# The last six sets of attention scores in two pairs of PSUM banks instead of one four-bank buffer, and a new list of the work

## The chip, the cores and the metric

The kernel runs on one core of one Trainium2 chip. The metric is the device time of one execution in microseconds (us), as the median of several runs. Beside it there is a profile of one execution; its span runs from the first to the last instruction. The engines are TensorE (PE in the profile; PEld is its loading of weights), VectorE (DVE), ScalarE (ACT), GpSimd (POOL) and SyncE (SP, which here only issues DMA transfers). Each of them works through its own instructions in the order in which they were issued.

## The reference

The input x has 2048 tokens of 640 features. Two attention layers of 32 heads with 20 features each read it, and a gate per token mixes their results.

```python
def reference(A_x, A_wqkv, A_w_phi, A_wo, B_x, B_wq, B_wk, B_wv, B_wo, B_beta, gate_w):
    ...
    # layer A: linear attention, features of a softmax of q and of -q
        phi_k = jnp.concatenate([_softmax(pk, axis=-1), _softmax(-pk, axis=-1)], axis=-1)
        kv = jnp.einsum('bhsf,bhsd->bhfd', phi_k, v)
        ...
        o = num / den
    ...
    # layer B: four segments of 512 tokens
        for s in range(N):
            ...
            logits = jnp.einsum('bhqd,bhkd->bhqk', qs, ks) * scale + mask
            p = _softmax(logits, axis=-1)
            a_dot = jnp.einsum('bhqk,bhkd->bhqd', p, vs)
            ...
            a_mem = num / den
            o = g * a_mem + (1.0 - g) * a_dot
            ...
            M = M + jnp.einsum('bhld,bhle->bhde', pk, vs)
    ...
    g = _sigmoid((x * gate_w).sum(-1, keepdims=True))
    return g * a + (1 - g) * b
```

## The kernel before, in words

**The list.** All work after the first loads is written as small steps in Python functions, and one long string, `ORDER` (line 847), says in which order they are issued. A word such as `P00` or `o1a` has a letter for the function (table `STEPS`, line 836), a digit for the step in it, and at the end a bank number or, with `a`, the wish that ScalarE does a copy in place of VectorE. How often a pair of letter and digit has come so far gives the number of the item, through the table `WHICH` where a step starts at another number or skips some. A helper (line 117) keeps each engine's instructions in the order of the list; that is why nearly all of the profile's rows carry line 117, and why they are told apart here by the names of their tiles. An engine that waits for something holds everything behind it.

**Layer B's attention** goes in groups of four heads: 4 segments of 8 groups, so groups 0 to 31. The scores of a pair of groups are computed as five sets (`scores`, line 595, letter `P`), 80 sets in all, numbers 0 to 79. A set fills four PSUM banks of 512 columns, one bank for each of four heads; keys stand on the 128 partitions and queries on the columns, and only the causal part is computed. Sets with number 0 or 3 in their five consist of one part, four matmuls with 32 rows (tile `st_ps`); those with 1, 2 or 4 consist of two parts, eight matmuls. Step 0 issues these matmuls, step 1 the exponential on ScalarE (tile `PT`, 128x2048), step 3 the causal masks on GpSimd (`affine_select` on `PT`): one mask in sets with number 0, 2 or 3 and two in those with 1 or 4.

There are eight banks. Four, with slots 0 to 3, are shared by all other work (`bank`, line 54). The other four begin as two pairs (`banks2`, line 61), which serve the folding of weights, the keys of layer A and the first three sets of scores (`NP = 3`); each of these sets has two exponentials of 1024 elements, steps 1 and 2, and its masks in steps 3 and 4. From set 3 on the four banks are one single buffer (`banks4`, line 64), so that the scores of one set wait until the exponential of the set before has read them.

The sums of the values weighted by `PT` (`attended_cols`, letter `U`, tile `uv_ps`) are turned by a DMA (`uN<-uT`) and normalized. In the last four groups (28 to 31, `UL = 28`) the letter `V` does it another way: forty matmuls with queries on the partitions (tile `nd_ps`; step 0 the part that needs no masks, step 4 the masked diagonal), normalized straight from PSUM (V1, V2, V3). `M` (memory) does the products with the running memory and adds both in `oB` (step 5).

**Layer A** projects q and k through weights into which the feature map is folded (`A`, `B`, `F`, `W`, and `f`, `d`, `n` for the queries: tiles `k_ps`, `v_ps`, `pf_ps`, `dn_ps`, `num_ps`). `k`, `K`, `v`, `q` are keys, features and values of layer B (`proj`, `q_ps`), and `Y` the features of its queries (`eq` on ScalarE). `T` turns x for the first 512 tokens, `L` lets a DMA do that for the others. `c` loads the ten parts of the output weights WoA and WoB, `l` turns 128 rows of both layers' results, and `o` does the output products of these rows (tile `o_ps`, ten matmuls for each half of 320 columns) and stores them.

**The tail.** The last 512 rows go another way. `t` and `b` turn layer A's and layer B's results at once (`b` in three transfers: the columns 0 to 383, 384 to 511, 512 to 639). For each block j of 128 rows, `p` does the products of the first three chunks of layer B, `a` all of layer A's, `e` and `z` those with the fourth and fifth chunk of layer B; `h` copies and stores. Blocks 0 and 3 use shared banks; blocks 1 and 2 use, as one four-bank tile `o2_ps` from `banks4`, the banks of the scores.

Of the kernel before, what the change touches and what calls it, by code (L numbers as in the profile page):

```python
# [7 lines left out]
ACT = mybir.ActivationFunctionType  # L8
# [7 lines left out]
def kernel(  # L16
# [29 lines left out]
    NP = 3  # L46

# [10 lines left out]
    early = ExitStack()  # L58
    ps2 = early.enter_context(tc.tile_pool(name="ps2", bufs=1, space=bass.MemoryType.PSUM))

    def banks2(name, slot):
        return ps2.tile([P, 2, 512], F32, name=name, tag=f"two{slot}", bufs=1)

    def banks4(name):
        if not hasattr(lt, "ps4"):
            early.close()
            lt.ps4 = ctx.enter_context(tc.tile_pool(name="ps4", bufs=1, space=bass.MemoryType.PSUM))
        return lt.ps4.tile([P, 4, 512], F32, name=name, tag="four", bufs=1)
# [526 lines left out]
    def scores(n, step, at, ev):  # L595
# [3 lines left out]
        if step == 0:  # L599
# [8 lines left out]
            if n < NP:  # L608
                pair = [banks2("st_ps", (at + u) % 2) for u in range(2)]
            else:  # L610
                t.ps = banks4("st_ps")
                pair = [t.ps[:, 0:2], t.ps[:, 2:4]]
# [7 lines left out]
        elif step < 3:  # L620
            if step == 1:
                t.all = bpt.tile([P, 4, 512], BF16, name="PT")
                t.PT = [t.all[:, 0:2], t.all[:, 2:4]]
            sca.activation(out=t.PT[step - 1] if n < NP else t.all,
                           in_=t.pair[step - 1] if n < NP else t.ps, func=ACT.Exp, scale=SCALE_B)
        else:
            PT, b = (t.PT[step - 3], 2) if n < NP else (t.all, 4)
            for v in ([PT.rearrange("p b (n q) -> p (b n) q", q=256)[:, :, 0:P]] if j == 2 else
                      [PT[:, :, d0:d0 + P] for d0 in ((0,) if j in (0, 3) else (0, 384))]):
                gps.affine_select(out=v, in_=v, pattern=[[0, 2 * b if j == 2 else b], [1, P]],  # L630
                                  compare_op=ALU.is_ge, fill=0.0, base=0, channel_multiplier=-1)
# [165 lines left out]
    def tail_mm(j, part, hs, at):  # L797
        t = item("tail", j)
        if part == 0 and j in (1, 2):
            if not hasattr(lt, "o2"):  # L800
                lt.o2 = banks4("o2_ps")
            t.ps = [lt.o2[:, 2 * j - 2 + h, 0:320] for h in range(2)]
# [23 lines left out]
    def tail_out(j, step, at, ev):  # L826
# [5 lines left out]
        else:  # L832
# [10 lines left out]
             **{f"M{j}": lambda i: i + G for j in range(2, 6)}, "p1": lambda i: 3 * i}  # L843
# [103 lines left out]
```

## Time and profile before

| | us |
|---|---|
| median of 3 runs | 287.55 (286.81 to 287.84) |
| profiled execution | 287.34 |
| its span | 285.6 |
| ScalarE: 77 exponentials of 128x2048 | 145.2 |
| ScalarE idle before these, waiting for scores | 14.9 |
| TensorE waiting for an exponential ahead of scores | 4.7 |

The times of the profile count from the start of the span. In the groups a row gives the busy time in total, the mean of one instruction in ns, and then the idle time of the engine just before such instructions with what ended most of it. In a timeline a row gives start, length, engine, the instruction, and in brackets how long the engine had been idle and what released it. The mean granted clock of TensorE is 0.998 of full speed.

By windows of the profile, columns being the stretch, its length, and the busy time and number of instructions on TensorE, of its weight loads, on VectorE, ScalarE and GpSimd, then clock, DMA share and GB/s:

```profile
250.00:260.00 10.00, 9.58 (x142) 6.89 (x134) 8.96 (x23) 8.34 (x6) 9.77 (x16) 1.00 0.53 107
260.00:270.00 10.00, 8.94 (x159) 6.32 (x156) 9.67 (x25) 9.04 (x7) 8.11 (x12) 1.00 0.67 139
270.00:280.00 10.00, 9.70 (x106) 7.19 (x106) 3.62 (x10) 2.63 (x3) 2.39 (x5) 1.00 0.13 29
280.00:285.60 5.60, 1.81 (x14) 1.08 (x11) 1.38 (x3) 0.93 (x3) 0.00 (x0) 0.88 0.33 117
```

### The profile page before, as it was taken

What the parts mean: (1) busy time and instruction counts of PE and PEld (TensorE: products, weight loads), DVE (VectorE), ACT (ScalarE), POOL (GpSimd) and SP (SyncE); (2) the same over time, 40 slices, a digit from 0 to 9 for tenths busy, and PEclk for the clock granted to TensorE, in tenths of its full rate; (3) what the DMA queues carried; (4) which work ended last, traced back from release to release, by engine and by line L of the source; (5) the groups of instructions that cost most, each with busy time, mean ns of one, the idle gap of its engine ahead of it and who ended that gap; (6) DMA issues with size and microseconds to landing.
All of it is one profiled execution on the core that took longest, in us unless ns stands there. A gap on an engine that the chain in (4) does not pass through costs nothing.

```text
span 285.6 us, 8511 instructions
## 1 busy us (share of the span) xinstructions
PE 272.6 (95%) x3371; PEld 173.4 (61%) x3393; DVE 237.2 (83%) x577; ACT 239.0 (84%) x259; POOL 183.0 (64%) x305
## 2 busy tenths in 40 slices
PE   7999999999999998999999999999999999999894
PEld 4777676677676545565556566455565556676673
DVE  5969999998889758999778989868999678999922
ACT  2489888897886999998998998999897997988902
POOL 8060000045445856798997799978899898999620
PEclk9999999999999999999999999999999999999999
DMA  7999960100111683356761624183474133564612
GB/s 223 282 239 210 147 149 22 37 2 2 39 21 25 167 116 76 70 108 118 136 97 39 142 63 102 51 128 80 90 83 98 22 92 74 110 118 79 153 38 92
DMA packets 79721, 28.11 MB, mean 98 GB/s; under 512 B 70081, under 2 KB 79681, under 8 KB 79681
## 3 DMA queue, kind: packets, MB, share of 16 engines
q1 hardware_dynamic: 78736, 26.84, 47.1%
q10 hardware_dynamic: 944, 0.74, 0.8%
q8 instruction: 26, 0.43, 0.6%
q14 instruction: 15, 0.11, 0.2%
HBM read 5.61 MB, written 2.62 MB: 29 GB/s over the span
## 4 chain that ended last, share of the span: by engine, by line
PE 67%; ACT 17%; DVE 6%; POOL 5%; issue 2%; DMA 1%; DVEq 0%; ACTq 0%
ACT PT L117 15%; PE proj L117 10%; PE o_ps L117 10%; PE v_ps L117 8%; PE k_ps L117 8%; PE st_ps L117 7%; PE pf_ps L117 5%; PE q_ps L117 5%; PE uv_ps L117 4%; POOL PT L117 2%; PE num_ps L117 2%; PE mem_ps L117 2%; POOL oA L117 2%; DMA WkB<-in_B_wk_dram 1%; PE zb_ps L117 1%
## 5 line engine op out<-in xcount | busy, mean ns | idle before, releaser
L117 ACT ACTIVATE PT<-st_ps 128x2048 bf16<-128x2048 f32 (+1 forms) x83 | 151.0, 1823 | 17.7 <-PE st_ps L117 15.7
L117 POOL TENSOR_SCALAR_AFFINE_SELECT PT<-PT 128x512 bf16<-128x512 bf16 (+2 forms) x116 | 78.9, 694 | 26.5 <-ACT PT L117 26.2
L117 PEld LDWEIGHTS <-xT 128*128 128x128 bf16 x640 | 59.9, 98 | 28.5 <-issue 4.3
L117 PE MATMUL st_ps<-qTp,kTs 32*128 32x384 bf16 (+3 forms) x512 | 31.8, 300 | 5.3 <-ACT PT L117 4.7
L117 ACT ACTIVATE Ek<-k_ps 128x640 bf16<-128x640 f32 x32 | 26.5, 893 | 5.3 <-PE k_ps L117 1.8
L117 POOL TENSOR_TENSOR oA<-t,t 128x320 bf16<-128x320 f32 x32 | 29.2, 914 | 1.3 <-DVE t L117 1.3
L117 DVE TENSOR_TENSOR t<-num_ps,dd 128x320 f32<-128x320 f32 x64 | 28.4, 478 | 0.8 <-PE num_ps L117 0.5
L117 POOL MEMSET qTp<- 128x4096 bf16 x1 | 3.5, 3512 | 39.3 <-ACT vA L117 39.3
L117 PEld LDWEIGHTS <-oT 128*128 128x128 bf16 x240 | 21.9, 98 | 9.8 <-issue 2.2
L117 PEld LDWEIGHTS <-kTs 32*128 32x128 bf16 (+1 forms) x552 | 14.9, 92 | 20.3 <-issue 16.0
L117 PE MATMUL proj<-WkB,xT 128*128 128x320 bf16 x160 | 25.7, 300 | 0.7 <-DVE xT L117 0.4
L117 PE MATMUL proj<-WvB,xT 128*128 128x320 bf16 x160 | 26.1, 300 | 0.0
L117 DVE TENSOR_REDUCE ksum<-Ek 128x64 f32<-128x1280 bf16 x16 | 23.1, 1455 | 2.4 <-ACT Ek L117 2.4
L117 PE MATMUL pf_ps<-xT,WqA 128*128 128x512 bf16 x91 | 24.3, 380 | 0.7 <-DVE uq L117 0.2
L117 PE MATMUL q_ps<-xT,WqB 128*128 128x512 bf16 x87 | 23.7, 380 | 0.9 <-issue 0.3
L117 PE MATMUL v_ps<-WvA,xT 128*128 128x320 bf16 (+1 forms) x160 | 24.2, 300 | 0.0
L117 PE MATMUL k_ps<-qTp,xT 128*128 128x320 bf16 x160 | 23.5, 299 | 0.0
L117 ACT ACTIVATE ET<-pf_ps 128x512 bf16<-128x512 f32 x40 | 21.9, 628 | 0.0
L117 POOL TENSOR_TENSOR oB<-td,tm 128x320 bf16<-128x320 f32 (+4 forms) x25 | 20.5, 824 | 1.2 <-DVE td L117 0.6
L117 DVE CAST uT<-uv_ps 128x512 bf16<-128x512 f32 x28 | 18.8, 670 | 2.4 <-PE uv_ps L117 2.2
L117 PE MATMUL uv_ps<-PT,vB 128*32 128x512 bf16 (+1 forms) x448 | 20.4, 302 | 0.2
L117 PE MATMUL o_ps<-WoA,oT 128*128 128x320 bf16 x120 | 20.3, 300 | 0.0
(114 smaller groups left out, 485.4 us busy)
## 6 DMA issues: line engine op xcount, KB each, us to landing
out_dram<-osb SPq DMA_DIRECT2D x12, 160.0 KB
qTp<-qd SPq DMA_DIRECT2D x8, 128.0 KB
WvB<-in_B_wv_dram SPq DMA_DIRECT2D x1, 800.0 KB
vA<-in_B_wq_dram SPq DMA_DIRECT2D x1, 800.0 KB
WvA<-in_A_wqkv_dram SPq DMA_DIRECT2D x1, 800.0 KB
WoA<-in_A_wo_dram SPq DMA_DIRECT2D x5, 160.0 KB
WoB<-in_B_wo_dram SPq DMA_DIRECT2D x5, 160.0 KB
qTp<-qd SPq DMA_DIRECT2D x8, 96.0 KB
```

What stands on the lines that cost most here:

```text
L117: return lambda *a, **k: kept(f(*a, **k))
```

## The change

The four banks now have three lives: two pairs for sets 0 to 2, one buffer of four banks for sets 3 to 73, and two pairs again for sets 74 to 79 (`NQ = 74`). The last six sets have two exponentials of 1024 elements each and their masks in halves (steps 3 and 4). The tail's blocks 1 and 2 take a pair each, slot 0 and slot 1, in place of the halves of one four-bank tile. `WHICH` gives the steps P2 and P4 the sets 0, 1, 2 and then 74 to 79. The list is written anew: it has six words each of P2 and P4 more, the bank numbers of 223 steps differ, and words have other places: among them the fourth turning of x (`T00`, ahead of the second projection of the keys), the loads of x (`L`), the ten loads of output weights (`c`, now all between set 11 and set 16), some projections, features and memory products around sets 4 to 33, and the order from set 69 to the end.

```diff
+    NQ = 74
...
-    def banks2(name, slot):
-        return ps2.tile([P, 2, 512], F32, name=name, tag=f"two{slot}", bufs=1)
+
+    def pool(part):
+        if part != pool.part:
+            if pool.part:
+                pool.now.close()
+            pool.part, pool.now = part, ctx.enter_context(ExitStack())
+            pool.ps = pool.now.enter_context(
+                tc.tile_pool(name=f"ps{part}", bufs=1, space=bass.MemoryType.PSUM))
+        return pool.ps
+
+    pool.part = 0
+
+    def banks2(name, slot, last=False):
+        return pool(3 if last else 1).tile([P, 2, 512], F32, name=name, tag=f"two{slot}", bufs=1)
...
+        return pool(2).tile([P, 4, 512], F32, name=name, tag="four", bufs=1)
+
+    def paired(n):
+        return n < NP or n >= NQ
...
-            if n < NP:
-                pair = [banks2("st_ps", (at + u) % 2) for u in range(2)]
+            if paired(n):
+                pair = [banks2("st_ps", (at + u) % 2, n >= NQ) for u in range(2)]
...
-            sca.activation(out=t.PT[step - 1] if n < NP else t.all,
-                           in_=t.pair[step - 1] if n < NP else t.ps, func=ACT.Exp, scale=SCALE_B)
-        else:
-            PT, b = (t.PT[step - 3], 2) if n < NP else (t.all, 4)
+            sca.activation(out=t.PT[step - 1] if paired(n) else t.all,
+                           in_=t.pair[step - 1] if paired(n) else t.ps, func=ACT.Exp, scale=SCALE_B)
+        else:
+            PT, b = (t.PT[step - 3], 2) if paired(n) else (t.all, 4)
...
-            if not hasattr(lt, "o2"):
-                lt.o2 = banks4("o2_ps")
-            t.ps = [lt.o2[:, 2 * j - 2 + h, 0:320] for h in range(2)]
+            o2 = banks2("o2_ps", at, True)
+            t.ps = [o2[:, h, 0:320] for h in range(2)]
...
+             **{f"P{j}": lambda i: i if i < NP else i - NP + NQ for j in (2, 4)}}
...
-        "T00 w0 T1 k01 T02 k1 T03 T1 T1 k00 T01 k1 k02 T1 k03 k1 k00 K0 K1 k1 k01 K2 k1 K0 k02 I0 "
+        "T00 w0 T1 k01 T02 k1 T03 T1 T00 T1 k01 T1 k1 k02 I0 k03 k1 k00 k1 K0 k01 K1 k1 K0 K2 k02 "
...
-        "n00 n13 o1 l0 M01 Y0 M5 P00 n2 o02 P1 Y1 P3 n3 M2 Y2 V00 n4 M3 o1a o2 V4 P3 U3 P00 M4 "
-        "M03 P1 o02 V1 U4 M2 U5 V2 M3 M5 o1 P00 P3 V3 o2 n01 P1 n12 M4 V00 n2 M5 V4 n3 n03 n11 V1 "
-        "n2 Y0 P00 V2 n4 n3 b0 o02 P1 Y1 P3 V3 Y2 n4 o1 Y0 Y1 P00 P3 t0 M03 P1 o01 Y2 M2 M00 M3 "
-        "o1 Y0 P3 P00 M4 V02 P1 M2 Y1 M5 V4 M3 o2 p01 Y2 p13 V1 P3 M4 P00 V2 P1 M00 V3 a0 M2 M5 "
-        "M3 p00 P3 b0 M4 V02 V4 p01 V1 V2 V3 a0 M5 b0 e0 e0 a0 p00 p12 z0 z1 e0 h0a h1 z0 z1 a0 "
-        "h0a h2 h1 h2 z0 z1 e0 h0a h1 z0 z1 h2 h0a h1 h2 ")
+        "M3 o01 P3 n2 n3 M4 n00 n4 n13 l0 o1 Y0 P00 Y1 o02 P1 P3 n2 n3 Y2 n4 V01 U3 o1 o2 V4 U4 "
+        "P00 P3 V1 M00 V2 P1 o03 U5 M2 M3 P2 M5 P00 o1 P3 V3 o2 n02 P1 M4 n13 P4 n01 n2 n10 M5 n3 "
+        "P2 V02 n2 V4 n3 P00 P3 b0 V1 o03 n4 V2 P1 P4 V3 P2 n4 P00 o1 P3 Y0 Y1 t0 o01 P1 P4 Y2 P2 "
+        "P3 P00 o1 Y0 Y1 P4 M00 P1 V02 Y2 o2 M2 V4 M3 M4 P2 p03 P3 V1 M5 p11 V2 Y0 P00 P4 Y1 M00 "
+        "P1 a0 V3 M2 Y2 P2 P3 M3 p00 P4 M4 V02 M5 V4 M00 p01 V1 M2 V2 M3 b0 V3 a0 M4 M5 b0 a0 e0 "
+        "p02 p10 e0 z0 z1 z0 h0a z1 h1 e0 h0a a0 h1 h2 h2 z0 z1 e0 h0a h1 z0 z1 h2 h0a h1 h2 ")
```

More of the change, by code (lines that the diff above doesn't have):

```diff
@@ L55, in bank @@
         return ps.tile(shape, dtype, name=name, tag=f"one{slot}", bufs=1)
-    early = ExitStack()
-    ps2 = early.enter_context(tc.tile_pool(name="ps2", bufs=1, space=bass.MemoryType.PSUM))
-    def banks2(name, slot):
-        return ps2.tile([P, 2, 512], F32, name=name, tag=f"two{slot}", bufs=1)
+    def pool(part):
[9 more added lines that the diff above has]
+        return pool(3 if last else 1).tile([P, 2, 512], F32, name=name, tag=f"two{slot}", bufs=1)
     def banks4(name):
[L65 to L68, printed above, removed]
+        return pool(2).tile([P, 4, 512], F32, name=name, tag="four", bufs=1)
+    def paired(n):
+        return n < NP or n >= NQ
     bres = ctx.enter_context(tc.tile_pool(name="bres", bufs=1))
@@ L842 @@
     WHICH = {**{f"V{j}": lambda i: i + UL for j in range(5)}, "k2": lambda i: 2 * i + 1, "o2": lambda i: 2 * i + 1, "S1": lambda i: 2 * i + 1,
-             **{f"M{j}": lambda i: i + G for j in range(2, 6)}, "p1": lambda i: 3 * i}
+             **{f"M{j}": lambda i: i + G for j in range(2, 6)}, "p1": lambda i: 3 * i,
+             **{f"P{j}": lambda i: i if i < NP else i - NP + NQ for j in (2, 4)}}
     ORDER = (
[61 rows of a table removed]
[61 rows of a table added]
     done = {}
```

108 rows, old and new, of the table ORDER are left out of this document.

## The prediction

> **What bounds the kernel now.** I read the page first, then the waits of TensorE, then the timelines of the last 30 us of TensorE, ScalarE, GpSimd and the DMA queue, then the groups by form, and last the stretch around 63 us, where the kernel before already works with pairs of banks.
>
> ```profile
> span 285.6 us, 8511 instructions
> PE 272.6 (95%) x3371; PEld 173.4 (61%) x3393; DVE 237.2 (83%) x577; ACT 239.0 (84%) x259; POOL 183.0 (64%) x305
> ...
> PE st_ps L117 <- ACT PT L117: 4.7, 16, 0.6
> ```
>
> TensorE is busy 272.6 of 285.6 us, so all that an edit of the order can win lies in 13.0 us of its idle time. By ten-microsecond windows, 1.7 us of that stand in the first window and 3.8 us after 280 us, where the last results are copied and stored. Of the rest, 4.7 us are waits of score matmuls for an exponential: the four-bank buffer is single, so scores of the next set wait for the whole exponential.
>
> ```profile
> 257.38 0.40 PE L117 MATMUL st_ps<-qTp,kTs 32*128 32x384 bf16 x8
> ...
> 259.81 0.40 PE L117 MATMUL st_ps<-qTp,kTs 32*128 32x512 bf16 x4 [0.42 <-ACT PT L117]
> ...
> 262.27 0.40 PE L117 MATMUL st_ps<-qTp,kTs 32*128 32x384 bf16 x8 [0.21 <-ACT PT L117]
> ...
> 264.70 0.40 PE L117 MATMUL st_ps<-qTp,kTs 32*128 32x256 bf16 x8 [0.57 <-ACT PT L117]
> ...
> 267.08 0.40 PE L117 MATMUL st_ps<-qTp,kTs 32*128 32x512 bf16 x4 [0.21 <-ACT PT L117]
> ...
> 269.52 0.40 PE L117 MATMUL st_ps<-qTp,kTs 32*128 32x384 bf16 x8
> ...
> 271.95 0.97 PE L117 MATMUL o_ps<-WoB,kTs 128*128 128x320 bf16 x6 [0.30 <-ACT PT L117]
> ```
>
> These are sets 74 to 79, the six that the change edits. They stand 2.43 us apart (12.14 us over five steps): 0.50 us from the start of the scores to the start of the exponential, 1.88 us of exponential, 0.05 us until the scores may start again. The idle times in the brackets add up to 1.71 us; by starts of matmuls the gaps are a little longer, about 2.5 us, since a drained pipeline counts as busy. After 271.95 TensorE runs without a gap to 281.8.
>
> ```profile
> 62.66 0.39 PE L117 MATMUL st_ps<-qTp,kTs 32*128 32x512 bf16 x4
> ...
> 63.12 1.94 ACT L117 ACTIVATE PT<-st_ps 128x1024 bf16<-128x1024 f32 x2
> ...
> 64.94 0.43 ACT L117 CAST vA<-v_ps 128x320 bf16<-128x320 f32 x1
> ...
> 260.34 1.88 ACT L117 ACTIVATE PT<-st_ps 128x2048 bf16<-128x2048 f32 x1 [0.58 <-PE st_ps L117]
> 262.11 0.62 ACT L117 ACTIVATE eq<-qTp 128x512 bf16<-128x512 bf16 x1
> ```
>
> ```profile
> L117 POOL TENSOR_SCALAR_AFFINE_SELECT PT<-PT 128x512 bf16<-128x512 bf16 x95 | 60.0, 646 | 19.4 <-ACT PT L117 19.2
> L117 POOL TENSOR_SCALAR_AFFINE_SELECT PT<-PT 128x1024 bf16<-128x1024 bf16 x15 | 16.6, 1104 | 4.5 <-ACT PT L117 4.5
> L117 POOL TENSOR_SCALAR_AFFINE_SELECT PT<-PT 128x256 bf16<-128x256 bf16 x6 | 2.4, 422 | 2.6 <-ACT PT L117 2.5
> ```
>
> These price the halves: what two halves cost ScalarE against one whole, and what two half masks cost GpSimd against one.
>
> **The parts of the change.**
>
> *Exponentials in halves.* Two of 1024 end 1.94 us after the first starts, one of 2048 takes 1.88; six sets cost ScalarE 6 x 0.06 = 0.4 us more, in a stretch where its gaps before the scores are about 0.5 us each. The Trainium skill (ScalarE: Activation LUTs, What ACT_TABLE_LOAD costs) speaks against splitting: it gives each ACTIVATE with immediate scale and bias 186 ns beside 0.833 ns an element, less 93 ns where two follow each other. By that the estimate would be 6 x 0.093 = 0.6 us; the rows make it 0.4, so the sum does not change.
>
> *Masks in halves.* Sets 74, 75, 76, 78 and 79 have eight masks of 512 elements, now sixteen of 256: 8 x (2 x 0.422 - 0.646) = 1.58 us. Set 77 has one of 1024, now two of 512: 2 x 0.646 - 1.104 = 0.19. GpSimd gets 1.77 us more. Between 257.4 and 273.2 us it idles 2.69 us now (0.31, 1.10, 0.48, 0.63 and 0.17 in its timeline), so this fits if the halves come when it is free. If that cover is gone, the third rival below has the price.
>
> *What the pairs free.* The scores of a set are issued as four matmuls (heads 0 to 3) per part, the first two into pair 0, the last two into pair 1. Matmuls go out in the order of the list, so the third one holds TensorE until the second exponential of the set before has ended. What becomes free early is thus two matmuls of a set. For the sets of one part (75 and 78) the first exponential can follow the other set's second one without a gap; for sets of two parts (76, 77, 79) pair 0 is complete only after the held matmul. So the wait is kept, and only ScalarE's gap shrinks. I follow the new list from set 74 (t = 0), with the starts of the rows: 0.33 us for a set of scores, 1.36 for a half output tile of ten matmuls, 1.0 for forty nd_ps, 0.75 for the twelve num_ps, 0.82 for six tail products, ScalarE 0.46 us behind the scores, 0.91 us for each half but for the last one's 1.02.
> - Set 75: TensorE comes at 1.87 (scores, one memory product, one output tile); pair 1 is free at 2.45. Stall 0.6, as now (0.42 by the row).
> - Set 76: four num_ps groups and the whole of group 29's nd_ps lie ahead; TensorE comes at 4.4, or 4.7 if the last mask of set 74 on GpSimd is late; pair 1 is free at 4.33. No stall.
> - Set 77: comes at 6.1 to 6.4, pair 1 free at 6.8: 0.4 to 0.7.
> - Set 78: comes at 8.5, pair 1 free at 9.2: 0.7.
> - Set 79: comes at 11.4 to 11.9 (nd_ps of group 30 waits up to 0.5 for set 77's masks), pair 1 free at 11.6: at most 0.2.
>
> Set 79 thus starts at 11.6 to 11.9 against 12.14. Behind it, the tail product that waited 0.30 us for all four banks now needs pair 0 alone, which is free when TensorE comes. The forty nd_ps of group 31 wait for the last mask (about 15.2) and end at about 15.6; now they end at 16.39, with one memory product of 0.15 us included that the new list puts behind them. Gain of the tail: 16.39 - 15.6 - 0.15 = 0.65 us. What is late next: group 31's last sum on VectorE ends about 2.6 us after its nd_ps (1.71 now, 273.77 to 275.48; three steps of a memory product, 0.9 us by their rows, are newly between), and the transfer of the last 128 columns lands some 2.3 us later, as it does now (275.5 to 277.8). That is t = 20.5; TensorE, with 5.05 us of products ahead of those that need it, gets there at 15.6 + 5.05 = 20.65. So the margin is 0.15 us, on VectorE and SP's queue.
>
> *The start.* Now the fourth transposition of x stands behind the projection that waits for a copy:
>
> ```profile
> 6.23 0.88 DVE L117 COPY xT<-tp_ps 128x640 bf16<-128x640 bf16 x2
> ...
> 6.77 0.85 PE L117 MATMUL proj<-WkB,xT 128*128 128x320 bf16 x5 [0.42 <-DVE xT L117]
> 7.46 0.44 PE L117 MATMUL tp_ps<-ident,phk 128*128 128x128 bf16 x5
> ```
>
> The new list puts it ahead. Its 0.28 us (7.46 to the next start, 7.74) fill that gap, if the last rows of x are there at 6.2. From 10 to 70 us TensorE idles 0.10 us in all, so the 0.28 stay gained. Between 0 (rows late) and 0.42 I take 0.28.
>
> *The list between.* Of the 443 entries that put work on TensorE, most keep their order; banks are renamed, and some 30 projections, feature products and memory products move between sets 4 and 33, and a few after set 69. TensorE's sum of work is the same. The ten weight loads of the output stage now stand together between sets 11 and 16. SP's queue is issuing 13.9 of 16.5 us there (93.5 to 110); up to the next transposition of uv it gets two loads more (about 0.5 us each), 1.0 us that its own gaps of 2.6 us must take; queries and keys behind it are needed from set 20 on. The trace can't price such moves. At best the waits for exponentials between 62 and 257 us vanish (4.7 - 1.4 = 3.3 us less), at worst they double (3.3 more). I take 0, since the work between consecutive sets is nearly the same in both lists.
>
> **Sum.** 285.6 - 0.65 - 0.28 = 284.7 us of span. The profiled execution took 287.34, so 1.74 lie around its span: 286.4. The median of the runs shown, 287.55, is 0.2 above that execution; the prediction against it is 287.55 - 0.93 = **286.6 us**.
>
> **The rivals.**
> *Full overlap.* If TensorE is held less than I think, ScalarE sets the pace: the last exponential ends at 0.47 + 6 x 1.83 + 3 x 0.53 (the three eq between) + 0.1 = 13.1 instead of 14.53, 1.4 less; without any stall of TensorE, 2.5 less. With 2.0 the run takes 287.55 - 2.0 - 0.28 = 285.3. For it: the 1.94 us row. Against it: the held third matmul. The Trainium skill (PSUM — Partial Sum Buffer, Engine vs sequencer instructions) says that matmuls start and complete in program order; the waits of the scores above, behind which all of TensorE stands, agree.
> *Nothing gained.* The stalls only move from between sets into them and the start's gap is the data's: 287.5. For it: the stalls of 75, 77 and 78 above are nearly as long as now. Against it: the freed tail product.
> *Masks bind: slower.* If GpSimd's 1.77 us find no gap (it is 98% busy from 250 to 260), the last mask ends at 273.2 + 1.8 = 275.0, group 31's nd_ps at 275.4, its last sum 2.6 later (1.71 and 0.9 of the memory product), its transfer lands 2.5 later at 280.5; the products that started at 278.66 slip 1.8, and the run takes 287.55 + 1.8 - 0.28 = 289.1. It costs from a delay above 0.15 us at the last mask (the margin) and turns the run slower than before from about 1.1 (0.15 and the 0.93 gained). Against it: the first half's masks start a microsecond earlier.
> *The middle loses.* A moved projection or load holds VectorE or a bank between 70 and 150 us: half of the upper bound, 1.7 us, less the 0.9 gained, 288.3, up to 290.
>
> **Chances.** Forecast 45%, full overlap (or as much won in the middle) 18%, nothing gained 14%, masks 9%, middle 14%. What can't be told from no change is 0.5%, 1.4 us: 286.1 to 289.0. Faster than that: the full overlap and about four in ten of the forecast's cases, 37%; slower: most of the masks' and half of the middle's cases and a few others, 17%; within: 46%. The forecast's own range is 285.4 to 287.6; with the others 284.4 to 289.3.
>
> **What would show it.** Right: sets 74 to 79 in less than 12 us, waits of st_ps still there and just ahead of the third matmul of a set; ScalarE's halves 0.91 us apart; the tail product behind set 79 without a wait; no gap ahead of the last tail products. Wrong: sets 11 us apart or less (full overlap); nd_ps waiting for masks by more than 0.6 us, or a gap of TensorE ahead of the last products (masks); new waits for VectorE or SP between 70 and 150 us (middle).

## The result, and the profile after

| | us |
|---|---|
| before, median of 6 runs | 287.44 (286.81 to 287.84) |
| changed, median of 6 runs | 288.22 (287.31 to 289.61) |
| ratio, 95% interval | 1.0034, 1.0017 to 1.005 |
| profiled execution of the changed kernel, its span | 287.31, 285.6 |

The changed kernel is slower by about 1 us (0.5 to 1.4 by the interval) where 0.9 us less was forecast. Its runs also lie further apart: 2.3 us, against 1.0 for the kernel before. The execution that was profiled is the shortest of the six, so this one profile shows little of the loss; the first experiment gives a second one, of a run of 289.72 us. The helper of nearly all rows is now line 127.

The head of the page after, and below it its waits (total us, times, longest us):

```profile
span 285.6 us, 8532 instructions
## 1 busy us (share of the span) xinstructions
PE 273.6 (96%) x3372; PEld 172.6 (60%) x3393; DVE 235.9 (83%) x575; ACT 240.1 (84%) x267; POOL 185.6 (65%) x314
```

```profile
ACT PT L127 <- PE st_ps L127: 15.1, 27, 1.0
...
PE st_ps L127 <- ACT PT L127: 4.8, 17, 0.5
...
DVE rden L127 <- DMA uN<-uT: 3.6, 5, 1.0
...
DVE kpads L127 <- DMA kTs<-kpads: 1.9, 1, 1.9
```

The waits of score matmuls for an exponential are as long in total as before (4.8, were 4.7). VectorE's waits for two kinds of transposition are more than before: `rden` for `uN` was 2.1 us in 3 waits, and a wait of `kpads` for `kTs` did not exist.

The last six sets in TensorE's timeline after:

```profile
257.75 0.40 PE L127 MATMUL st_ps<-qTp,kTs 32*128 32x384 bf16 x8
...
259.70 0.39 PE L127 MATMUL st_ps<-qTp,kTs 32*128 32x512 bf16 x2
260.25 0.39 PE L127 MATMUL st_ps<-qTp,kTs 32*128 32x512 bf16 x2 [0.17 <-ACT PT L127]
...
262.67 0.40 PE L127 MATMUL st_ps<-qTp,kTs 32*128 32x384 bf16 x8
...
264.46 0.28 PE L127 MATMUL st_ps<-qTp,kTs 32*128 32x256 bf16 x2
265.15 0.39 PE L127 MATMUL st_ps<-qTp,kTs 32*128 32x256 bf16 x6 [0.41 <-ACT PT L127]
...
266.94 0.39 PE L127 MATMUL st_ps<-qTp,kTs 32*128 32x512 bf16 x2
267.50 0.39 PE L127 MATMUL st_ps<-qTp,kTs 32*128 32x512 bf16 x2 [0.17 <-ACT PT L127]
...
269.91 0.40 PE L127 MATMUL st_ps<-qTp,kTs 32*128 32x384 bf16 x8
...
271.76 0.98 PE L127 MATMUL o_ps<-WoB,kTs 128*128 128x320 bf16 x6
```

In sets 75, 77 and 78 two score matmuls go out and the third waits, as forecast; the tail product at 271.76 has no wait (it had 0.30). From set 74 to set 79 it is 12.16 us, were 12.14.

To see where time goes in a list of 1600 steps, the first score matmul of each of the 80 sets was read from the traces, as time since the first matmul, and set against the kernel before. This table gives the difference in us (negative: earlier than before); "end" is the start of the last matmul. The columns behind the first two belong to experiments below.

| set | changed | changed, again (e1) | e5 | e14 | e6 | e13 |
|---|---|---|---|---|---|---|
| 0 | -0.33 | +0.42 | -0.34 | -0.33 | +0.59 | +0.47 |
| 18 | -0.58 | +0.21 | -0.59 | -0.60 | +0.59 | +0.47 |
| 24 | -0.58 | +1.73 | +1.12 | -0.59 | +0.59 | +0.47 |
| 38 | -0.48 | +1.53 | +0.92 | -0.26 | +0.59 | +0.46 |
| 43 | +0.02 | +2.45 | +0.93 | -0.26 | +0.51 | +0.47 |
| 69 | -0.23 | +2.20 | +0.70 | -0.22 | +0.43 | +0.22 |
| 70 | +0.41 | +2.83 | +1.33 | -0.16 | +0.43 | +0.22 |
| 74 | +0.38 | +2.80 | +1.30 | -0.21 | +0.43 | +0.22 |
| end | -0.04 | +2.37 | +0.86 | -0.47 | -0.26 | -0.48 |

Three places lose: between sets 18 and 24 in some runs only (0 in the one profile, 1.5 in the other), between 38 and 43 (0.5 and 0.9), and from 69 to 70 (0.6 in both). The tail behind set 74 gains 0.4.

The profile of before has a delay of its own that the table shows as a gain of all others: at set 59 every other kernel comes 0.25 us nearer to it (e6 0.09), e8 too, which there has the list of before. VectorE waits 0.36 us for `uN` at 216.27 in that profile, behind a store that takes SP 1.82 us to issue; in e8 the same store takes 1.13 and nothing waits.

### The profile page after: what moved, and what is told of

The parts are those of the page before. It is cut to its first block, busy times and chain, and to the rows that moved or that the text cites. A ratio compares the mean times of both kernels' runs of the same rounds, so it can differ in the third digit from the quotient of the medians.

```text
span 285.6 us, 8532 instructions
## 1 busy us (share of the span) xinstructions
PE 273.6 (96%) x3372; PEld 172.6 (60%) x3393; DVE 235.9 (83%) x575; ACT 240.1 (84%) x267; POOL 185.6 (65%) x314
## 3 DMA queue, kind: packets, MB, share of 16 engines
HBM read 5.61 MB, written 2.62 MB: 29 GB/s over the span
## 4 chain that ended last, share of the span: by engine, by line
PE 65%; ACT 21%; DVE 7%; issue 3%; POOL 1%; DVEq 0%; ACTq 0%
ACT PT L127 17%; PE o_ps L127 10%; PE proj L127 9%; PE v_ps L127 8%; PE k_ps L127 8%; PE st_ps L127 6%; PE pf_ps L127 5%; PE q_ps L127 5%; PE uv_ps L127 3%; ACT ET L127 2%; PE kv_ps L127 2%; PE num_ps L127 2%; PE mem_ps L127 2%; DVE t L127 2%; PE nd_ps L127 1%
## 5 line engine op out<-in xcount | busy, mean ns | idle before, releaser
L127 POOL TENSOR_SCALAR_AFFINE_SELECT PT<-PT 128x512 bf16<-128x512 bf16 (+2 forms) x125 | 81.4, 667 | 66.1 <-ACT PT L127 65.6
L127 PE MATMUL st_ps<-qTp,kTs 32*128 32x384 bf16 (+3 forms) x512 | 32.8, 300 | 5.2 <-ACT PT L127 4.8
L127 PE MATMUL o_ps<-WoB,oT 128*128 128x320 bf16 x120 | 20.2, 299 | 0.0
L127 DVE CAST uT<-uv_ps 128x512 bf16<-128x512 f32 x27 | 18.1, 672 | 2.0 <-PE uv_ps L127 1.9
```

The source lines that it names most:

```text
L127: return lambda *a, **k: kept(f(*a, **k))
```

## The experiments

Each ratio is to runs of the kernel before on the same chip (287.1, 287.6, 287.5 and 287.2 us for e1 to e4, e5 to e8, e9 to e12 and e13 to e16), with its 95% interval. The diffs give words of the list; bank numbers are renamed where two lists meet.

| run | median us | ratio |
|---|---|---|
| e1 changed, again | 289.17 | 1.0057 (1.0031 to 1.0083) |
| e2 new only from set 44 | 287.17 | 1.0003 (0.999 to 1.0016) |
| e3 new only up to set 44 | 288.11 | 1.003 (1.0014 to 1.0045) |
| e4 ten loads spread | 288.66 | 1.0049 (1.0033 to 1.0066) |
| e5 sets 36 to 39 as before | 287.43 | 1.0008 (0.9991 to 1.0025) |
| e6 pairs only | 287.08 | 0.9984 (0.9972 to 0.9996) |
| e7 start and new tail | 286.78 | 0.9974 (0.9963 to 0.9984) |
| e8 before, loads bunched | 287.85 | 1.0025 (0.9999 to 1.0051) |
| e9 three places back | 288.01 | 1.0022 (1.001 to 1.0034) |
| e10 changed, two loads | 289.64 | 1.0064 (1.0047 to 1.0082) |
| e11 e7, two loads | 287.16 | 0.9989 (0.9979 to 0.9998) |
| e12 e7, pair by pair | 286.85 | 0.9981 (0.997 to 0.9992) |
| e13 start and pairs only | 286.35 | 0.9967 (0.9956 to 0.9978) |
| e14 e9 with loads cut | 287.1 | 0.9993 (0.9984 to 1.0003) |
| e15 changed, loads cut | 288.45 | 1.004 (1.0027 to 1.0053) |
| e16 e9, ten late loads | 287.12 | 0.999 (0.9981 to 0.9999) |

### Which half: e1, e2, e3

e1 is the changed kernel once more. e2 and e3 cut both lists at set 44, where both have issued the same steps, and join them crosswise.

```diff
 e2:  words up to set 44
-  of the changed list
+  of the list before (the rest, with the pairs, stays changed)
 e3:  words from set 44 on
-  of the changed list
+  of the list before (no pairs at the end)
```

> The changed kernel as it is, once more. Its six runs lay between 287.3 and 289.6 us, while those of before lay between 286.8 and 287.8; its profiled execution was one of the short ones (span 285.6, the same as before). Theory A (a variable delay: some transfer or wait is late in part of the executions) expects the same wide spread, two groups about 1.5 to 2 us apart, and a ratio of about 1.003. Theory B (a small constant loss) expects a spread as narrow as before's, 1 us, around 288.2.

> The list of before up to set 44, from there the changed list with the pairs for the last six sets. The profile of the changed kernel shows +0.33 us gained at the start, +0.4 lost at set 70 and at sets 74 and 76, and an end equal to before. If the loss and the spread come from the new tail with its pairs: 288.2 to 288.5 with a spread of 2 us. If they come from the head (loads of output weights bunched, other order of the early transfers): 287.4 to 287.8 with a spread of 1 us.

> The changed list up to set 44, from there the list of before, with the single four-bank buffer to the end. Opposite of the run before: if the tail is the cause, 287.1 to 287.4 with a spread of 1 us; if the head is, 288.0 to 288.5 with a spread of 2 us.

The new first half without the pairs costs 0.3%, the new second half with them nothing that can be told from zero. So the loss is mainly in the first half, and the second half gives back about what the pairs win. The spread is in the first half too: the runs of e1 lie within 2.9 us and those of e3 within 2.2, those of e2 within 1.1.

### The query feature at set 38: e5

In sets 36 to 39 the new list moves the features of two groups of queries (`Y`, item 7 and 8) ahead of a feature of keys (`K`, item 10). e5 puts only this stretch of 40 words back, in which 12 differ.

```diff
-Y0 P00 Y1 q03 P3 P1 M4 n2 n3 v02 Y2 n4 q1 n01 Y0 n10 P00 Y1 ... o1 K0 K1 U4 P00 ...
+K0 P00 K1 q03 P3 P1 M4 n2 n3 v02 K2 n4 n01 q1 Y0 n10 P00 Y1 ... o1 Y0 Y1 P00 U4 ...
```

> The changed kernel with the stretch between sets 36 and 39 in the order of before: there the changed list computes the key features (ek) two sets later and two query features (eq) a set earlier each, and the second of these reads queries whose transfer has just been issued. In the long execution of the changed kernel sets 38 to 43 lose 0.9 us against before, in the short one 0.5. If that early eq is one of the causes: no wait of eq for qTp, these sets on the grid of before, and the median 0.5 to 0.9 us below the changed kernel's (287.3 to 288.4), still wide. If it is not: 288.2 to 289.2 as the changed kernel.

The words name banks as in the changed list; "..." is what both have in the same or nearly the same order. e5 came to 1.0008, against 1.0034 and 1.0057 for the changed kernel: 0.7 to 1.4 us, with intervals of 0.5 us and more to either side. In the table its step from set 38 to 43 is 0.0 (+0.92, +0.93), so the traces price the step at 0.5 to 0.9. The place in the timeline of the changed kernel's second run (e1):

```profile
162.64 0.61 SPq L127 DMA_DIRECT2D qTp<-qd  x1
...
163.45 1.88 ACT L127 ACTIVATE PT<-st_ps 128x2048 bf16<-128x2048 f32 x1
165.86 0.63 ACT L127 ACTIVATE eq<-qTp 128x512 bf16<-128x512 bf16 x1 [0.54 <-DMA qTp<-qd]
...
168.63 0.40 PE L127 MATMUL st_ps<-qTp,kTs 32*128 32x384 bf16 x8 [0.59 <-ACT PT L127]
```

The transfer that brings the queries is issued at 162.64, and the exponential that reads them starts 3.2 us later, with ScalarE idle for 0.54. The copy and the exponential of set 38 stand behind it on ScalarE, so set 39's scores wait 0.59 in their turn. In the first profile after the same step starts 3.3 us behind its transfer (160.40 to 163.71; it names VectorE's `qd`, which had ended just then, as what ended the wait of 0.40), in e15 also 3.3 (161.32 to 164.61). In the list before it stands a set later: it starts at 166.29, 4.75 us behind its transfer at 161.54, and doesn't wait.

### The pairs and the start by themselves: e6, e7, e12, e13

e6 takes the list of before and adds only the pairs: `P2` behind each `P1` and `P4` behind each `P3` from set 74 on, and the tail's blocks 1 and 2 each in a pair. e7 takes the list of before, T00's set early, and the changed list from set 75. e12 is e7 with the score matmuls issued pair by pair; e13 is the list of before with the early T00 and e6's pairs.

```diff
 e6, e13: in the last six sets
-P1 ... P3
+P1 P2 ... P3 P4
 e7, e13: at the start (T0, fourth time)
-T03 T1 T1 k00 T01 k1 k02 T1
+T03 T1 T00 T1 k01 T1 k1 k02
 e12: in scores()
-for (col, c, kT, qT) in parts:
-    for i in range(4):
+heads = [(p, i) for p in parts for i in range(4)]
+if n >= NQ:
+    heads.sort(key=lambda t: t[1] // 2)
+for (col, c, kT, qT), i in heads:
```

> The list of before as it is, with nothing but the pairs: each of the last six sets in two exponentials and half masks, next to each other at the places they have now, and the two pairs for the tail's blocks. My forecast's arithmetic says that pairs shorten sets 74 to 79 by a few tenths and free the first tail product: 286.6 to 287.0. If the third matmul's wait takes all of it: 287.1. If the nine more masks bind: over 287.6, with nd_ps waiting for masks.

> What the runs so far point to as the good parts: the list of before, with the fourth turning of x early (0.33 us less at set 0 in the trace) and the changed list only from set 75 on, so without the stretch around set 69 to 70, where the changed tail loses 0.6 us before the pairs give 0.45 back. If each part adds: 287.1 - 0.3 - 0.4 = 286.4. If the start's gain drowns in what varies there from run to run: 286.7.

> The kernel of e7 with the score matmuls of each of the last six sets issued pair by pair: all parts of heads 0 and 1 first, then all of heads 2 and 3. If the third matmul's wait for the second bank pair is what keeps ScalarE idle between the halves: sets 76, 77 and 79 start earlier, and 0.2 to 0.5 us less than e7, 286.2 to 286.6 at 287.5. If two matmuls side by side in place of four cost TensorE as much as four: the first half's scores come no sooner, the second half's later, and the time is 287 to 288.

> The list of before with two edits only: T00's set ahead of the projection at the start, and the exponentials and tail's products of the last six sets in pairs of banks, in the order of before. The pairs alone gave a ratio of 0.9984 and a profile 0.69 us shorter behind set 59; the start is worth about 0.3. If the two add up: 286.3 to 286.7 us at 287.5 for the kernel before, ratio 0.996 to 0.9975. If the start's gain is lost in how the first matmuls run: 286.9 to 287.2.

From set 74 to the end e6 gains 0.69 us (+0.43 to -0.26 in the table) and e13 0.70; the changed kernel's new order of the same steps gains only 0.42, and e7 and e12 0.26 and 0.25. The gain of the two edits by themselves is e13's: 0.9967, that is 0.95 us, the lowest ratio of all kernels here, though the interval of e7 overlaps it. Its sets 74 to 77 on TensorE:

```profile
257.59 0.40 PE L127 MATMUL st_ps<-qTp,kTs 32*128 32x384 bf16 x8
...
260.42 0.49 PE L127 MATMUL num_ps<-KV,ET 128*128 128x140 bf16 x6
...
262.25 0.40 PE L127 MATMUL st_ps<-qTp,kTs 32*128 32x384 bf16 x8
...
264.73 0.39 PE L127 MATMUL st_ps<-qTp,kTs 32*128 32x256 bf16 x6 [0.41 <-ACT PT L127]
```

Set 76 comes 4.66 us behind set 74, in the changed kernel 4.92, though the same twelve `num_ps` and forty `nd_ps` lie between: the order of before has six `num_ps` ahead of the `nd_ps` and six behind them, which take 0.77 us together, the new list all twelve in a row, which take 1.00 with two short pauses that no row names.

e12 missed: with the third matmul no longer in the way the median is e7's (286.85 and 286.78), and set 79 starts 12.32 us behind set 74 in both. ScalarE's timeline of e12 says why:

```profile
262.75 1.94 ACT L127 ACTIVATE PT<-st_ps 128x1024 bf16<-128x1024 f32 x2 [1.19 <-PE st_ps L127]
264.57 0.63 ACT L127 ACTIVATE eq<-qTp 128x512 bf16<-128x512 bf16 x1
265.09 1.94 ACT L127 ACTIVATE PT<-st_ps 128x1024 bf16<-128x1024 f32 x2
266.90 0.65 ACT L127 ACTIVATE eq<-qTp 128x512 bf16<-128x512 bf16 x1
267.42 1.96 ACT L127 ACTIVATE PT<-st_ps 128x1024 bf16<-128x1024 f32 x2
```

From 262.75 on ScalarE has no idle time: an exponential and an `eq` in turn set the pace of sets 76 to 78, and the scores wait for nothing that TensorE could do sooner. What is left idle, the 1.19 us ahead of set 76, is the work that the list puts before that set.

### The bunched loads: e4, e8, e10, e11

The ten loads of output weights stand between sets 11 and 16 in the new list. e4 puts them back behind the words that they follow in the list before; e8 moves only them, in the kernel before. e10 and e11 make two loads of the ten, in the changed kernel and in e7.

```diff
 e10, e11 (and e9): in load_o()
-W, w = ((lt.WoA, A_wo), (lt.WoB, B_wo))[n // KC]
-syn.dma_start(out=W[:, n % KC, :], in_=rows5(w)[:, n % KC, :])
+if n % KC == 0:
+    W, w = ((lt.WoA, A_wo), (lt.WoB, B_wo))[n // KC]
+    syn.dma_start(out=W, in_=rows5(w))
 e4: in the list
-... c0 P00 M6 c0 f03 P1 c0 U3 c0 M02 q00 M6 c0 ... (ten c0 by set 16)
+... five c0 there, five between sets 22 and 30, as in the list before
```

> The changed kernel with the ten loads of output weights put back to the places they have before, behind the same neighbours; nothing else moved. If SP's queue between 94 and 107 us, which they crowd (a copy of keys waits 1.9 us there for a transposition), is what delays some executions: 287.2 with a spread of 1 us. If not: 288.2 with a spread of 2 us, as the changed kernel.

> The kernel before with nothing changed but the ten loads of output weights, issued where the changed list has them (between sets 11 and 16). If the loads on SP's queue are what makes part of the executions long (sets 18 to 24 lose 1.5 us in the long ones, behind waits of VectorE for turned uv): 287.5 to 288.5 with a wide spread. If they only hurt together with the other moves: 287.1 and a spread of 1 us.

> The changed kernel with its ten output-weight loads merged into two of the same total bytes, at the same stretch. If SP's time for issuing is what delays the transpositions of the normalised vectors: no loss at sets 18 to 24, no run beyond 288.6, median 287.6 to 288.2 (the eq at set 38 and the stretch at set 69 are left). If the bytes' traffic is the cause: runs up to 289 to 290 as in the changed kernel, median 288.2 to 289.

> The kernel of e7 (list of before, the early T00, the new tail from set 75) with the ten output-weight loads merged into two. If the ten loads still cost something where they stand in the list of before: 286.3 to 286.6 at 287.5 for the kernel before. If they are hidden there: 286.7 to 286.9 as in e7. If a whole matrix in one transfer holds up a transposition behind it: over 287.

VectorE's timeline in the changed kernel's second run:

```profile
101.98 0.49 DVE L127 CAST kpads<-proj 128x320 bf16<-128x320 f32 x1 [2.20 <-DMA kTs<-kpads]
...
108.17 0.25 DVE L127 RECIPROCAL rden<-uN 128x16 f32<-128x16 bf16 x1 [1.66 <-DMA uN<-uT]
...
113.19 0.25 DVE L127 RECIPROCAL rden<-uN 128x16 f32<-128x16 bf16 x1 [0.87 <-DMA uN<-uT]
```

In the kernel before none of these steps waits for a transfer; here VectorE stands for 4.7 us in three places. From 108 to 120 us it is busy 10.96 of 12, so what it is late comes through to TensorE, whose timeline has:

```profile
113.78 0.84 PE L127 MATMUL proj<-WkB,xT 128*128 128x320 bf16 x5 [1.18 <-DVE dd L127]
```

Sets 18 to 24 lose 1.5 us. In the first profile after the waits are 1.94, 0.98 and none, and nothing is lost. Over six profiles the loss goes with the second wait: none at 0.98 and 1.12 us (first profile, e9), 1.4 to 1.7 at 1.25 to 1.70 (e10, e5, e1, e3). e8, with the loads alone, had eight runs at 286.9 to 288.0 and four at 289.1 to 290.9: a loss that comes by chance, of 0.25% on the median with an interval that just reaches zero. Its profile is of one of the eight and shows no loss at these sets, so what makes the four long is not shown.

e4 didn't settle it: its sets 18 to 24 lose nothing, but sets 24 to 32 lose 0.8 (0.1 in the profile after), and there `rden` waits 1.53 us for `uN`; of the 0.8, half comes by set 28, where nothing waits for a transfer and e9, e14 and e15 lose 0.33 as well, and 0.41 at set 32, right behind this wait. e10 refuted that the time of issuing is the price: two issues in place of ten, and the kernel has the highest median of all (its interval overlaps e1's). In e11 the two loads do about what ten do (0.9989 against e7's 0.9974, intervals that overlap).

### What is left when all three are put back: e9, e14, e15, e16

e9 is the changed kernel with sets 36 to 39 and the order from set 69 to set 74 as before, the pairs behind them, and two merged loads. e14 is e9, and e15 the changed kernel, with the loads cut to the first fifth of each matrix, which every output product then reads. e16 is e9 with the ten loads singly or by twos behind transpositions from set 14 to 27.

```diff
 e14, e15: in load_o(); in outputs() and tail_mm() every Wo[:, c, ...] becomes Wo[:, 0, ...]
-syn.dma_start(out=W[:, n % KC, :], in_=rows5(w)[:, n % KC, :])
+if n % KC == 0:
+    syn.dma_start(out=W[:, 0, :], in_=rows5(w)[:, 0, :])
 e16: in the list
-c0 x10 between sets 11 and 16
+U2 c0 (items 4, 5) ... U2 c0 c0 (items 6 to 9)
```

> The changed kernel with three places of its list put back: the ten output-weight loads become two whole-matrix loads, sets 36 to 39 are issued in the order of before, and from set 69 to the last six sets the list of before stands, with the pairs of banks behind it. If the three places (SP's queue at 93 to 112 us, the early query feature at set 38, the stretch at sets 69 to 72) are all of the loss: 286.6 to 287.0 us at 287.5 for the kernel before, no rden wait over 1 us near 108 us, no eq wait near set 38, and set 70 no later against before than set 69. If something else in the changed list costs time too: 287.3 or more, and the curve of set starts shows a further step.

> Leaves work out: of each output-weight matrix only the first fifth is loaded (320 KB in place of 1600 KB), and every output product reads that fifth; the number of matmuls stays. The list is the changed one with sets 36 to 39 and the order from set 69 as before, and the pairs at the end. If the bytes of the bunched loads are the rest of the loss: 286.5 to 287.0 at 287.5 for the kernel before, no VectorE wait for a transposition over 0.5 us between 90 and 118 us. If another part of the changed list costs time: 287.5 to 288.

> Leaves the same work out of the changed kernel and is otherwise its list. If the bytes of the loads delay the transpositions: 1 to 1.5 us less than the changed kernel, 287.3 to 287.8 (the query feature at set 38 and the stretch at set 69 are left), no loss at sets 18 to 24, and runs within 1 us of each other. If their place on SP's queue or something else does: 288.2 to 289.2 as in the changed kernel.

> The list of the run with three places put back, with the ten loads one or two at a time, each right behind a transposition of normalised vectors, from 109 to 143 us. If a load costs time only where a transposition stands behind it: 286.6 to 287.1 at 287.5 for the kernel before. If loads anywhere in the changed list delay the transpositions that come later, as the spread loads did at set 28: 287.5 to 288.5, with a wait of rden for uN over 1 us at 115 to 150 us.

e9 is not the 286.6 to 287.0 us that were expected: it is still 0.22% slower than before. e9 and e14 have the same list and the same number of transfers; e14's two loads have 160 KB each in place of 800. The difference is 0.29%, 0.8 us. In their two profiles 0.34 of it lies between sets 0 and 24. SP's queue in e9, and then in e14:

```profile
95.01 0.50 SPq L127 DMA_DIRECT2D WoB<-in_B_wo_dram  x1
95.57 5.68 SPq L127 DMA_TRANSPOSE kTs<-kpads  x2
101.35 2.95 SPq L127 DMA_DIRECT2D qTp<-qd  x4
104.41 1.22 SPq L127 DMA_TRANSPOSE uN<-uT  x1
```

```profile
94.43 0.41 SPq L127 DMA_DIRECT2D WoB<-in_B_wo_dram  x1
94.89 2.62 SPq L127 DMA_TRANSPOSE kTs<-kpads  x2
97.71 2.96 SPq L127 DMA_DIRECT2D qTp<-qd  x4
101.50 6.55 SPq L127 DMA_TRANSPOSE uN<-uT  x2
```

Two transpositions of keys take SP 2.62 us to issue behind 320 KB, and 5.68 behind 1600 KB. In these 5.68 us the DMA engines are busy 0.96 of the time. So SP itself is held while the loads' bytes are under way, and all that stands behind it starts later: counted from the second load, the four transfers of queries come after 6.3 us in place of 3.3, the next `uN` after 9.4 in place of 7.1. (The 6.55 in the last row is a gap between two transpositions, merged.) e16 shows that with all the bytes another place is enough: ten whole loads behind the transpositions give 0.999, as good as a fifth of the bytes ahead of them. (Against e9 it also has ten loads in place of two; ten loads ahead of the transpositions were not run in this list.)

e15 gives the other half of the account. Its expectation, 1 to 1.5 us less than the changed kernel, failed: sets 18 to 24 lose nothing and no transposition of keys is waited for, but with the loads cut the changed kernel is still at 1.004. So the bytes of the ten loads cost its median 0 to 0.5 us; e15 and e14 differ by the query feature and the stretch at set 69, and by 0.47%, 1.35 us.

The stretch at set 69 in the changed kernel, and in e14 with the order of before:

```profile
244.89 0.33 PE L127 MATMUL mem_ps<-Mbd,phiq 128*128 128x84 bf16 x4
245.05 0.54 PE L127 MATMUL num_ps<-KV,ET 128*128 128x80 bf16 x6
245.87 0.84 PE L127 MATMUL o_ps<-WoA,oT 128*128 128x320 bf16 x5 [0.28 <-DVE uT L127]
```

```profile
244.90 0.49 PE L127 MATMUL num_ps<-KV,ET 128*128 128x80 bf16 x6
245.30 0.84 PE L127 MATMUL o_ps<-WoA,oT 128*128 128x320 bf16 x5
```

The new list puts a memory product there (0.16 us) and gives the output product a bank whose last user, the sum `uv_ps`, VectorE is still copying out. The output tile starts 0.98 us behind the first row instead of 0.40; set 70 comes 0.6 us later in every kernel with this stretch (changed, e1, e2, e4, e5, e10, e15) and in none without it. By medians it is e2 against e6, 0.19% or 0.55 us, in which the weaker tail of the new order is included.

What is left between e14 (0.9993) and e13 (0.9967), 0.75 us, is by the two profiles 0.44 in the tail's order (0.26 gained behind set 74 in place of 0.70) and 0.36 between sets 0 and 69 (0.11 lost, where e13 gains 0.25, which is the delay of before at set 59). The second part is 0.33 by set 28 and 0.29 at set 64, less 0.27 that the new order gains up to set 18. At 28 VectorE's `t` and at 64 ScalarE's exponential start some 0.3 us later behind matmuls whose rows show no gap. The changed kernel itself has neither loss; the one at 64 comes in all six kernels that have the new first half with the loads issued otherwise (e4, e9, e10, e14, e15, e16). Why stays open.

## Why the prediction was wrong

**The sum without the list.** The tail's 0.65 and the start's 0.28 make 0.93 us. The kernel that has just these two edits, e13, is 0.95 us faster (0.63 to 1.26). So both mechanisms work; that the sums agree so closely is in part luck, since the 0.65 was worked out for the new order of the tail, where it measured 0.42.

**The tail.** In the order of before the pairs gain 0.69 and 0.70 us, forecast 0.65. The steps hold in the rows: the third matmul waits, the halves come 0.9 us apart, the tail product needs pair 0 alone, and no gap opens ahead of the last products. In the new order, of which the forecast spoke, sets 74 to 79 take 12.16 us in place of 11.6 to 11.9, and the gain is 0.42. The mis-sized term is TensorE's arrival at set 76: 4.92 us behind set 74 by the starts, forecast 4.4 to 4.7. The twelve `num_ps` measured 1.00 (forecast 0.75, from 260.58 to 261.58) and the forty `nd_ps` 1.09 (1.0, to 262.67). What I took for the obstacle, the held third matmul, costs nothing behind set 76, as e12 shows.

**The masks.** GpSimd's 1.77 us more found room: its busy time rose even by 2.6 us in the whole span, and no `nd_ps` of the last groups waits for a mask. This rival fell.

**The start.** The wait of 0.42 for VectorE's copy is gone in every kernel with the early T00, and set 0 comes 0.33 us earlier in the profile after, forecast 0.28. A single profile proves little, because the start itself varies by more (last section). Profiles whose first projection took as long can be compared: at 1.54 us set 0 stands at +0.42 to +0.47 with the early T00 (e1, e13, e15) and at +0.59 and +0.79 without (e6, e8); at 0.84 to 0.91 us at -0.31 on average in seven profiles with it and at 0 in the one without (before). That is 0.25 to 0.3 us.

**The list between.** This is the step that failed: "I take 0, since the work between consecutive sets is nearly the same in both lists." The list loses what e13 gains and 1.0 to 1.6 us more, 1.9 to 2.6 us in all, inside the bound of 3.3. Nearly the same work between two sets is no measure, since what a moved step costs is the wait that it meets: a query feature 3.2 us behind its transfer (0.5 to 0.9 by the traces, 0.7 to 1.4 by the medians), an output product in a bank not yet copied out (0.6 with the memory product ahead of it), a transposition's issue behind large loads (0 to 1.5, by the run), and the last six sets in the new order (0.3). The rival "the middle loses", at 14%, named this kind of mechanism, and its sign, new waits of VectorE between 70 and 150 us, is there (1.94 and 0.98 in the first profile). It named the time that came, 288.3, by luck: that is half an upper bound, and it looked only between 70 and 150 us, while the two losses that come in every profile with these words stand at 163 and 245. And for SP's queue the forecast counted 0.5 us for each load and not what the loads do to the transpositions behind them.

## What to carry to other kernels

Where a list is written anew for the sake of one edit, run that edit on the old list as well: here it was worth 0.95 us, and the new list cost twice as much or more. For each step that has moved, read from the trace when its input lands and when its bank was last read, and not only how much work lies between its neighbours. Put large loads behind the small transfers that somebody waits for, not ahead of them; making two large loads of ten did not help in either kernel in which it was tried.

## What the runs showed of the hardware

**A transposition's issue can be held.** On SP's queue it mostly takes 1.2 to 1.3 us (56 of 77 in the kernel before); behind two loads of 800 KB two of them took 5.68 us. The issues of the four plain transfers right behind were not stretched (2.95 and 2.96 us for four).

**TensorE's first matmuls vary from run to run.** The first projection in the profile after, and in e1, the same kernel:

```profile
4.66 0.85 PE L127 MATMUL proj<-WkB,xT 128*128 128x320 bf16 x5
5.35 1.12 PE L127 MATMUL tp_ps<-ident,phk 128*128 128x128 bf16 x15
```

```profile
4.82 1.54 PE L127 MATMUL proj<-WkB,xT 128*128 128x320 bf16 x5
6.15 1.39 PE L127 MATMUL tp_ps<-ident,phk 128*128 128x128 bf16 x15
```

Five equal matmuls take 0.85 us in one and 1.54 in the other, while the granted clock reads 1.00 in both. In the eighteen profiles of this study they took 0.84 to 0.91 in eight and 1.06 to 1.54 in ten, with old and new starts alike. With what follows this moves set 0 by 0.75 us (-0.33 and +0.42 in the table), nearly as much as the edits are worth; a profile's end is not to be compared with another's without it. The Trainium skill (TensorE: Matmul & The Clock Gate, What's actually happening) says that TensorE starts at half its clock and is released by a window of some 3.4 us that runs on its own, so that the moment differs from run to run; the two durations, nearly one to two, agree with it, and the profile's granted clock doesn't show it.
